# RWKV-7 attention and a squared-ReLU FFN on one core: weights rounded through PSUM with ACT's help, stores issued after their producers, the state's decay and transposes moved into the iteration before

## The chip, the cores and the metric

The kernel runs on one core of one Trainium2 chip. The metric is the device time of one launch in microseconds. The kernel before took 1444.61 us, the median of three runs (1443.46 to 1452.1). The profile is one further execution.

Engines: PE is TensorE's matmuls, PEld its weight loads, DVE is VectorE, ACT is ScalarE, POOL is GpSimd, SP is SyncE, which here only issues DMAs. A trailing q (SPq, ACTq) is an engine's own issuing of DMAs. Each engine works through its instructions strictly in the order in which the program lists them.

## The reference

```python
# attention: B=4, H=8, S=768, D=40; r, k, v, w, a, b of shape (B,H,S,D), w in 0.85..0.95
for t in range(S):
    y[:, :, t] = einsum('bhd,bhde->bhe', rt, state)          # state: (B,H,D,D), starts at 0
    Sa = einsum('bhde,bhe->bhd', state, at)
    state = state * wt[:, :, None, :] - einsum('bhd,bhe->bhde', Sa, bt)
    state = state + einsum('bhd,bhe->bhde', vt, kt)
# bridge: x = y as (B*S, H*D) = (3072, 320)
# FFN: w_in (320, 2048), w_out (2048, 320), both float64 as given
h = maximum(x @ w_in, 0.0)
out = (h * h @ w_out).astype(float32)
```

## The kernel before

*The attention in chunks.* The 768 steps are cut into 6 chunks of 128. A chunk of one batch, with its 8 heads, is a unit; `order` lists the 24 units, chunk by chunk and in each the four batches. A unit has four pieces of work, each a Python generator that yields between its steps:

- `early(i)` (through `prepare(i)`, which first issues the next unit's loads): products of the decays w in both directions (`up`, `down`), the transposed and scaled a and b, their products N. All are stored to DRAM: `kept_up`, `kept_down`, `kept_a`, `kept_d` (the diagonal blocks of N, which `solve` reads) and `kept_n`.
- `solve(c)`: POOL inverts the 64-row blocks of a whole chunk, four units at once, with 63 pairs of TENSOR_TENSOR (L298, L300), and stores the result to DRAM as `kept_t`. Its input `half_n` comes back from `kept_d`.
- `rest(i)`: loads down, aT, up of unit i and later `T` (from `kept_t`, four DMAs, L344) and `N21`; forms the masked products A and RV and the scaled k and b.
- `chain(i)`: what depends on the state. It scales the state `st` by the decays (L359 to L362, DVE), transposes it (L366, PE, into PSUM tile ps_c, copied by ACT to `sd`), multiplies through T and N (copies xr and minus_x by ACT; L378 is the first of them), grows the state, and writes y into `tokens`. Rows that don't fit are moved by small DMAs from SP, the gap copies (L428).

*The FFN.* `ffn()` takes two units of tokens as a group (12 groups): 16 w_in steps (three matmuls into PSUM ps_f, ACT Relu L445, DVE square L446) and 8 w_out steps of four matmuls each; the output is copied by ACT (`o`, L459) and stored by SP (L461).

*The weights.* They come as float64 pairs of 32-bit words, and the kernel rounds them to fp32 with integer operations: 12 wide pieces of w_in (128x512) and 16 narrow ones of w_out (128x320). `fetch_weights()` issues a piece's DMAs on ACT's queue into one of two raw buffers, `rounded()` does eight DVE instructions (L180 to L188). The wide raw buffers lie in the still unused w_out tile, so rows name that `w_out`.

*What sets the order.* Nothing is scheduled automatically: instructions stand on their engines in the order of the Python code. First come eight units of `early`, with `solve(0)` after the fourth, then most of `rest(0)`, then `run(weights(...))` with 16 pieces, `solve(1)`, and the 24 iterations. `weave` interleaves in iteration i: chain(i), rest(i+1), prepare(i+8), weights (iterations 0 and 1), and 13 steps of the FFN. After the last unit of chunk c, solve(c+2) is issued. Then the remaining FFN runs alone. The line `first = rest(0, ...)` stops `rest(0)` after six of its seven steps, so its T loads come behind the rounding in the code, though SP reaches them early.

A DMA of SP's or ACT's queue announces its landing on one of eight semaphores (DMAHW0_49 to DMAHW7_49), which the framework hands out in program order over both queues; a DMA that takes one again waits until the one that had it before has landed. PSUM has 8 buffers of 128x512: four `ps_w`, two `ps_c`, two `ps_f`.

Of the kernel before, what the change touches and what calls it, by code (L numbers as in the profile page):

```python
# [9 lines left out]
I32 = mybir.dt.int32  # L10
# [7 lines left out]
def kernel(  # L18
# [66 lines left out]

    quads = lambda t_: t_.rearrange("p (q t) -> p q t", q=NP)
# [70 lines left out]
    spare = [room[:, 2 * WI * i:2 * WI * (i + 1)] for i in range(2)]  # L157
    spare_bits = [room[:, WI * i:WI * (i + 1)].bitcast(I32) for i in (4, 5)]
    raws = [single(f"raw{i}", [128, 2 * DM]) for i in range(2)]
    raw_bits = [single(f"bits{i}", [128, DM]).bitcast(I32) for i in range(2)]  # L160
    fetched = []

    def fetch_weights():
        if not pieces:
            return
        dst, srcs, cleared = pieces.pop(0)
        wide = len(pieces) >= NF
        raw = (spare if wide else raws)[len(pieces) % 2]
        if cleared:
            nc.vector.memset(raw, 0.0)  # L170
        for row, m_, src in srcs:
            nc.scalar.dma_start(out=raw.bitcast(I32)[row:row + m_], in_=src.bitcast(I32))
        fetched.append((dst, raw, spare_bits if wide else raw_bits))

    def rounded(dst, raw, scratch):
        power, p_ = scratch
        words = raw.rearrange("p (f e) -> p f e", e=2)
        lo, hi = words[:, :, 0].bitcast(U32), words[:, :, 1].bitcast(I32)
        bits = dst.bitcast(I32)
        nc.vector.tensor_scalar(power, hi, 20, 0x7FF, Alu.logical_shift_right, Alu.bitwise_and)  # L180
# [5 lines left out]
        nc.vector.scalar_tensor_tensor(rest, lo, 2.0 ** -52, p_.bitcast(FP32), Alu.mult, Alu.mult)  # L186
        nc.vector.tensor_tensor(bits, bits, p_, Alu.bitwise_or)  # L187
        nc.vector.tensor_tensor(dst, dst, rest, Alu.add)  # L188
# [3 lines left out]
    for j in range(NT):  # L192
        for f in range(0, DFF, WI):
            srcs = [(row, n, moe_w_in[o:o + n, f:f + WI]) for j_, row, o, n in places if j_ == j]
            pieces.append((w_in[:, j, f:f + WI], srcs, f < 2 * WI and sum(n for _, n, _ in srcs) < 128))
    pieces += [(w_out[:, f, :], [(0, 128, moe_w_out[f * 128:(f + 1) * 128, :])], False) for f in range(NF)]

    def weights(n):
        for _ in range(n):
            if moe_w_in.dtype == FP32:  # L200
                if pieces:
                    dst, srcs, _ = pieces.pop(0)
                    if sum(m_ for _, m_, _ in srcs) < 128:
                        nc.gpsimd.memset(dst, 0.0)
                    for row, m_, src in srcs:
                        nc.scalar.dma_start(out=dst[row:row + m_], in_=src)
            else:
                fetch_weights()
                if fetched:
                    rounded(*fetched.pop(0))  # L210
            yield
# [36 lines left out]
    def early(i):  # L248
# [11 lines left out]
        nc.sync.dma_start(out=kept_up[i], in_=up)  # L260
        nc.sync.dma_start(out=kept_down[i], in_=down)
        yield
        bT, aT = turned("bT", 1), turned("aT", 1)
        nc.vector.tensor_tensor(bT, bT_, down[:, :, 1:C + 1], Alu.mult)
        nc.vector.tensor_tensor(aT, aT_, up[:, :, :C], Alu.mult)  # L265
        nc.sync.dma_start(out=kept_a[i], in_=aT)
        yield
        bb, c = order[i]
        for e, p_ in enumerate(products(bT, aT)):
# [3 lines left out]
            for half in range(2):  # L273
                rows = slice(half * HC, (half + 1) * HC)
                nc.sync.dma_start(out=kept_d[c][bb, half, heads].rearrange("h s t -> s h t"), in_=t_[rows, :, rows])
            nc.sync.dma_start(out=kept_n[i][:, heads, :], in_=t_[:HC, :, HC:])
# [29 lines left out]
    def rest(i, g):  # L306
# [7 lines left out]
        ends = g["ends"] = new("ends", [128, NP], 3)  # L314
        g["up"], g["aT"] = up, aT
        yield
        kT, rT = turned("kvT", 1), turned("rT", 2)
        nc.vector.tensor_tensor(kT, turn(x_["k"]), down[:, :, 1:C + 1], Alu.mult)  # L318
        nc.vector.tensor_copy(ends, down[:, :, 0])
        yield  # L320
        g["A"] = masked("A", 4, kT, aT)
# [5 lines left out]
        yield  # L327
        g["RV"] = masked("RV", 4, vT, rT)
# [4 lines left out]
        inv = p_.rearrange("t (h d) -> t h d", h=H)[:, :, :D]  # L333
        for nm in ("k", "b"):
            nc.vector.tensor_tensor(x_[nm][:, :, :D], inv, x_[nm][:, :, :D], Alu.mult)
            g[nm] = x_[nm]
        g["v"] = x_["v"]
        yield

        g["T"], g["N"] = new("T", [128, H, HC], 2), new("N21", [HC, H, HC], 2)  # L340
        nc.sync.dma_start(out=g["N"], in_=kept_n[i])
        for half in range(2):
            for par in range(2):
                nc.sync.dma_start(out=g["T"][half * HC + par:(half + 1) * HC:2],  # L344
# [222 lines left out]
```

## Time and profile before

| | |
|---|---|
| median of three runs | 1444.61 us |
| the profiled execution | 1453.09 us, span on the core 1451.4 us |
| mean granted TensorE clock | 0.808 of full |
| busy: PE | 1049.5 us (72%) |
| busy: POOL | 687.7 us (47%) |
| busy: DVE | 591.8 us (41%) |
| busy: ACT | 201.6 us (14%) |
| first solve on POOL | 57 to 175 us |
| first xr copy of the first chain | 321.94 us |
| last FFN run, nothing beside it | from 1410.39 us |

How to read it: a busy TensorE isn't one at its peak, since its matmuls take twice as long at half the granted clock. The rows called stretches below give the busy time of each engine in a stretch with the clock granted in it. A wait row reads: engine, what waited, what released it, total us, times, longest. Idle time of an engine that isn't the bottleneck costs nothing. The slices cut the span into 40 of 36 us.

### The profile page before, as it was taken

The page shows a single profiled execution, that of the slowest core. Times are in us where ns is not written, and L with a number is a line of the kernel's source. Part 1 is how long each engine was busy: PE and PEld are TensorE (multiplying, and loading weights), DVE is VectorE, ACT ScalarE, POOL GpSimd, SP SyncE. Part 2 cuts the span into 40 slices and gives each one's busy share as a digit, 9 for nine tenths or more (in the row PEclk, how much of TensorE's full clock was granted, in tenths as well). Part 3 has the DMA queues.
Part 4 walks back from the last instruction along what each step waited for, and adds up shares of the span by engine and source line. Part 5 has one row for each costly group of instructions (what it writes and reads, how often), then busy time and mean ns, then how long its engine had stood idle before and what let it go on. Part 6 is the DMA issues. An engine that isn't in the chain of part 4 may idle for free.

```text
span 1451.4 us, 18536 instructions
## 1 busy us (share of the span) xinstructions
PE 1049.5 (72%) x7248; PEld 865.5 (60%) x7248; DVE 591.8 (41%) x1095; ACT 201.6 (14%) x453; POOL 687.7 (47%) x815
## 2 busy tenths in 40 slices
PE   5340000016699689898998998989968989899999
PEld 4340000016577578676876876768757767686877
DVE  6433059998653252333332532344223123232311
ACT  1000000001022121211110211111111111121211
POOL 2399859991000099920699503997009991000000
PEclk7555555556589998998897997988898799989999
DMA  9960091103554544451744248514343133320200
GB/s 166 180 136 14 31 161 37 45 27 115 128 99 89 99 83 84 89 128 55 114 99 93 72 88 121 99 53 107 82 83 53 42 58 82 62 53 21 54 11 10
DMA packets 300104, 116.91 MB, mean 81 GB/s; under 512 B 270192, under 2 KB 275184, under 8 KB 298480
## 3 DMA queue, kind: packets, MB, share of 16 engines
q1 hardware_dynamic: 295104, 98.94, 35.6%
q10 hardware_dynamic: 4048, 10.49, 2.6%
q0 software_dynamic: 864, 6.29, 1.1%
q8 instruction: 57, 0.93, 0.3%
q14 instruction: 31, 0.25, 0.1%
HBM read 75.96 MB, written 38.73 MB: 79 GB/s over the span
## 4 chain that ended last, share of the span: by engine, by line
PE 63%; DVE 15%; POOL 8%; DMA 8%; SPq 3%; issue 2%; ACT 1%; DVEq 0%; POOLq 0%; ACTq 0%
PE ps_f L78 34%; PE ps_c L78 16%; PE ps_w L78 6%; POOL half_t L300 4%; PE ps_w L226 4%; POOL half_p L298 4%; DMA in_k<-in_k_dram 2%; DMA half_n<-kept_d 1%; DMA tokens<-tokens 1%; PE ps_c L366 1%; SPq L428 1%; DVE w_in L187 1%; DVE w_out L184 1%; DVE w_out L186 1%; DMA kept_a<-aT 1%
## 5 line engine op out<-in xcount | busy, mean ns | idle before, releaser
L298 POOL TENSOR_TENSOR half_p<-half_n,half_t 128x462 f32<-128x462 f32 (+19 forms) x378 | 316.2, 836 | 465.3 <-DMA half_n<-kept_d 436.1
L300 POOL TENSOR_TENSOR half_t<-half_t,half_p 128x462 f32<-128x462 f32 (+19 forms) x378 | 346.8, 917 | 29.6
L78 PE MATMUL ps_f<-tokens,w_in 128*128 128x256 f32 x1152 | 322.3, 427 | 25.9 <-DMA tokens<-tokens 25.3
L78 PEld LDWEIGHTS ps_f<-tokens,w_in 128*128 128x128 f32 x1152 | 232.6, 213 | 69.1 <-issue 21.4
L78 PE MATMUL ps_f<-w_out,hid 128*128 128x320 f32 x768 | 225.4, 443 | 0.0
L446 DVE TENSOR_TENSOR hid<-ps_f,hid 128x256 f32<-128x256 f32 x192 | 80.4, 420 | 350.9 <-ACT hid L445 350.9
L78 PE MATMUL ps_c<-xr,T 64*64 64x40 f32 x768 | 59.8, 239 | 216.8 <-ACT xr L378 215.0
L78 PEld LDWEIGHTS ps_c<-xr,T 64*64 64x64 f32 x768 | 54.0, 148 | 236.1 <-ACT xr L378 215.1
L78 PEld LDWEIGHTS ps_f<-w_out,hid 128*128 128x128 f32 x768 | 142.7, 193 | 56.1 <-issue 2.7
L445 ACT ACTIVATE hid<-ps_f 128x256 f32<-128x256 f32 x192 | 73.8, 384 | 377.1 <-PE ps_f L78 377.1
L78 PEld LDWEIGHTS ps_c<-in_v,A 128*128 128x128 f32 x384 | 66.0, 259 | 3.0 <-issue 0.2
L78 PE MATMUL ps_c<-in_v,A 128*128 128x40 f32 x384 | 63.0, 337 | 0.0
L318 DVE TENSOR_TENSOR kvT<-ps_w,down 128x512 f32<-128x512 f32 x24 | 16.6, 691 | 101.6 <-DMA down<-kept_down 91.5
L242 DVE TENSOR_TENSOR A<-ps_w,upper 128x512 f32<-128x512 f32 x48 | 30.9, 685 | 61.6 <-PE ps_w L78 61.6
L78 PE MATMUL ps_w<-aT,bT 40*128 40x128 f32 x384 | 35.1, 334 | 25.5 <-DVE aT L265 25.5
L366 PE MATMUL ps_c<-ident,state 128*128 128x128 f32 x80 | 17.7, 361 | 47.9 <-DVE state L362 47.9
L242 DVE TENSOR_TENSOR RX<-ps_w,upper 128x512 f32<-128x512 f32 x48 | 30.9, 685 | 51.2 <-PE ps_w L78 51.2
L378 ACT COPY xr<-ps_c 64x320 f32<-64x320 f32 x24 | 10.1, 419 | 292.9 <-DVE bits L186 220.9
L78 PEld LDWEIGHTS ps_w<-aT,bT 40*128 40x128 f32 x384 | 29.6, 230 | 32.4 <-issue 23.1
L226 PE MATMUL ps_w<-ident,in_k 128*128 128x128 f32 x96 | 20.0, 343 | 37.1 <-DMA in_k<-in_k_dram 37.1
L366 PEld LDWEIGHTS ps_c<-ident,state 128*128 128x128 f32 x80 | 11.3, 178 | 57.8 <-DVE state L362 45.6
L271 ACT COPY N<-ps_w 128x512 f32<-128x512 f32 x48 | 25.9, 589 | 137.3 <-PE ps_w L78 120.4
(184 smaller groups left out, 1325.6 us busy)
## 6 DMA issues: line engine op xcount, KB each, us to landing
kept_up<-up SPq DMA_DIRECT2D x24, 260.0 KB
kept_down<-down SPq DMA_DIRECT2D x24, 260.0 KB
down<-kept_down SPq DMA_DIRECT2D x24, 260.0 KB
up<-kept_up SPq DMA_DIRECT2D x24, 260.0 KB
kept_a<-aT SPq DMA_DIRECT2D x24, 256.0 KB
kept_d<-N SPq DMA_DIRECT2D x96, 64.0 KB
half_n<-kept_d SPq DMA_DIRECT2D x12, 512.0 KB
kept_t<-half_t POOLq DMA_DIRECT2D x6, 1024.0 KB, 4.6
```

The source lines that it names most:

```text
L78: nc.tensor.matmul(o, l_, r_, start=start, stop=True, skip_group_check=True)
L184: nc.vector.scalar_tensor_tensor(p_, hi, -(1 << 31), power, Alu.bitwise_and, Alu.bitwise_or)
L186: nc.vector.scalar_tensor_tensor(rest, lo, 2.0 ** -52, p_.bitcast(FP32), Alu.mult, Alu.mult)
L226: nc.tensor.transpose(p_[:, q * 128:(q + 1) * 128], pair(x_, q), ident)
L242: nc.vector.tensor_tensor(t_, p_, over4(upper), Alu.mult)
L271: nc.scalar.copy(t_, p_)
L298: eng.tensor_tensor(p_, ns[s // Q][:, s % Q, s % Q + 1:].unsqueeze(1).to_broadcast([128, n, m_]), ts[:, :n, s:s + 1].to_broadcast([128, n, ...
L300: eng.tensor_tensor(ts[:, :n, s + 1:], ts[:, :n, s + 1:], p_, Alu.subtract)
L318: nc.vector.tensor_tensor(kT, turn(x_["k"]), down[:, :, 1:C + 1], Alu.mult)
L366: nc.tensor.transpose(p_[:, q * 128:(q + 1) * 128], st[:, q].rearrange("p e d -> p (e d)"), ident)
L445: nc.scalar.activation(h_, p_, Act.Relu)
L446: nc.vector.tensor_tensor(h_, p_, h_, Alu.mult)
```

## The change

1. **Rounding.** Intermediate words go to PSUM (`bits` in ps_f, `low` in ps_c during the first run, in ps_f later), so that each DVE instruction has at most one input in SBUF. Six DVE instructions are left per piece; two go to ACT (L213: Relu with the bias tile `lowest`, which clamps and shifts the exponent; L214: the low word scaled by 2^-52). Four wide raw buffers instead of two; POOL clears them once. Pieces whose sources are two DMAs (j = 2) come first, and the first fetches stand ahead of rest(0)'s ACT copies. In the first run one piece's first half is issued ahead of the previous piece's second half. 12 wide and 5 narrow pieces are rounded ahead of the first chain, where it was 12 and 4; 11 are left for iterations 0 and 1.
2. **Stores.** `store()` puts a DMA into a line; `tick()`, once in each weave step, issues those that are due: one or two steps after the producer's code.
3. **State.** The decay and the transposes of the state move from chain(i)'s head to rest(i) in the iteration before. T and N are loaded earlier for the last three batches of a chunk. rest has nine steps, woven from step 2 on.
4. **FFN.** A group may start one iteration later than before: group 0 after iteration 1 as before, group g after iteration 2g+2. Iteration 4 so has no FFN, and behind the last chain stand 35 steps instead of 23.
5. **Buffers.** aT in `early` 1 to 2; A 4 to 2; f 2 to 1; end 2 to 1; ends 3 to 2; sd 1 to 2.

```diff
+    def later(fn, steps=2):
+        line.append([steps, fn])
+    def tick():
+        for entry in line:
+            entry[0] -= 1
+        while line and line[0][0] <= 0:
+            line.pop(0)[1]()
+    def store(out_, in_, steps=2):
+        later(lambda: nc.sync.dma_start(out=out_, in_=in_), steps)
...
     def fetch_weights():
...
+        while count[0] < len(pieces):
+            n = count[0]
+            wide = n < NARROW
+            if len(fetched) + len(begun) >= (4 if wide else 2) or (n >= NARROW and count[1] < NARROW):
+                return
...
+    def rounded_first(pool):
...
+        bits, low = psum(ps_f)[:, :m_], psum(pool)[:, :m_]
+        p_ = (wide_p if m_ == WI else narrow_p)[(len(begun) + count[1]) % 2]
+        nc.vector.tensor_scalar(bits.bitcast(I32), hi, 20, 0x7FF, Alu.logical_shift_right, Alu.bitwise_and)
+        nc.scalar.activation(bits.bitcast(I32), bits.bitcast(I32), Act.Relu, bias=lowest, scale=float(1 << 23))
+        nc.scalar.activation(low, lo, Act.Copy, scale=2.0 ** -52)
+    def rounded_second():
...
+        nc.vector.scalar_tensor_tensor(p_bits, hi, -(1 << 31), bits, Alu.bitwise_and, Alu.bitwise_or)
         nc.vector.tensor_scalar(bits, hi, 0xFFFFF, 3, Alu.bitwise_and, Alu.logical_shift_left)
-        nc.vector.tensor_scalar(power, power, 896.0, 1151.0, Alu.max, Alu.min)
-        nc.vector.tensor_scalar(power, power, 896.0, float(1 << 23), Alu.subtract, Alu.mult)
-        nc.vector.scalar_tensor_tensor(p_, hi, -(1 << 31), power, Alu.bitwise_and, Alu.bitwise_or)
-        rest = power.bitcast(FP32)
-        nc.vector.scalar_tensor_tensor(rest, lo, 2.0 ** -52, p_.bitcast(FP32), Alu.mult, Alu.mult)
-        nc.vector.tensor_tensor(bits, bits, p_, Alu.bitwise_or)
-        nc.vector.tensor_tensor(dst, dst, rest, Alu.add)
+        nc.vector.tensor_tensor(dst, low, p_, Alu.mult)
+        nc.vector.tensor_tensor(bits, bits, p_bits, Alu.bitwise_or)
+        nc.vector.tensor_tensor(dst, sum_, dst, Alu.add)
...
-        nc.sync.dma_start(out=kept_up[i], in_=up)
+        store(kept_up[i], up)
...
+        if c > 0:
+            st = states.tiles[bb]
+            f_ = new("f", [128, NP, 2], 1)
+            nc.vector.tensor_tensor(f_[:, :, 0], ended[bb], ends, Alu.mult)
...
+            nc.vector.tensor_tensor(st[:, :, :, :D], st[:, :, :, :D],
+                                    f_.unsqueeze(3).to_broadcast([128, NP, 2, D]), Alu.mult)
         g["RV"] = masked("RV", 4, vT, rT)
...
+        if c > 0:
+            p_ = psum(ps_c)
+            for q in range(NP):
+                nc.tensor.transpose(p_[:, q * 128:(q + 1) * 128], st[:, q].rearrange("p e d -> p (e d)"), ident)
+            sd = g["sd"] = new("sd", [128, NP, 2, DP], 2)
+            nc.scalar.copy(sd.rearrange("p q e d -> p q (e d)"), quads(p_))
+        yield
+        if bb == 0:
+            inverses()
...
+    run(weights(NARROW + NF // 4, ps_c))
+    while begun:
+        rounded_second()
...
-        if i % GB == GB - 1:
-            gathered.add(i // GB)
+        if i % GB == 0 and i > 0 or i == GB - 1:
+            gathered.add(max(i // GB - 1, 0))
+    gathered.add(len(order) // GB - 1)
```

Where the rows come to stand. First ACT's queue around the first solve: L172 (L201 after) are the DMAs that fetch weights, 40 + 40 + 24 + 16 rows to a piece or 40 + 40 for the first four after, L323/L325 (L371/L373) the copies of rest(0), L213/L214 the new rounding instructions. Before, from the copies on:

```order
L323 COPY rT<-ps_w 128x512 [waits PE_49]
L325 COPY kvT<-ps_w 128x512 [waits DVE_49,PE_49]
L172 DMA w_out<-in_moe_w_in_dram 40x1024 [waits DMAHW7_49,DVE_49]
L172 DMA w_out<-in_moe_w_in_dram 40x1024 [waits DMAHW1_49]
L172 DMA w_out<-in_moe_w_in_dram 24x1024 [waits DMAHW3_49]
L172 DMA w_out<-in_moe_w_in_dram 16x1024 [waits DMAHW5_49]
L172 DMA w_out<-in_moe_w_in_dram 40x1024 [waits DMAHW7_49,DVE_49]
L172 DMA w_out<-in_moe_w_in_dram 40x1024 [waits DMAHW1_49]
L172 DMA w_out<-in_moe_w_in_dram 24x1024 [waits DMAHW2_49]
L172 DMA w_out<-in_moe_w_in_dram 16x1024 [waits DMAHW4_49]
```

The same place now; eight DMAs of the first four pieces (40x1024) stand ahead of the copies and are not shown:

```order
L213 ACTIVATE ps_f<-ps_f,lowest 128x512 [waits DVE_49]
L214 ACTIVATE ps_c<-w_out 128x512
L201 DMA w_out<-in_moe_w_in_dram 40x1024 [waits DMAHW0_49,DVE_49,Activation_49]
L201 DMA w_out<-in_moe_w_in_dram 40x1024 [waits DMAHW2_49]
L201 DMA w_out<-in_moe_w_in_dram 24x1024 [waits DMAHW4_49]
L201 DMA w_out<-in_moe_w_in_dram 16x1024 [waits DMAHW6_49]
L213 ACTIVATE ps_f<-ps_f,lowest 128x512 [waits DVE_49]
L214 ACTIVATE ps_c<-w_out 128x512 [waits DMAHW7_49]
L201 DMA w_out<-in_moe_w_in_dram 40x1024 [waits DMAHW0_49,DVE_49,Activation_49]
L201 DMA w_out<-in_moe_w_in_dram 40x1024 [waits DMAHW2_49]
L201 DMA w_out<-in_moe_w_in_dram 24x1024 [waits DMAHW3_49]
L201 DMA w_out<-in_moe_w_in_dram 16x1024 [waits DMAHW5_49]
```

Before, the second piece's third and fourth DMAs take semaphores that T loads had; now these are the sixth piece's, and ACT's rounding instructions stand between the DMAs. SP's loads of T (from kept_t, which POOL's queue writes, DMASW0_49) and of the second solve's input, before:

```order
L344 DMA T<-kept_t_247 32x8x64 [waits DMAHW0_49,DMASW0_49]
L344 DMA T<-kept_t_247 32x8x64 [waits DMAHW2_49]
L344 DMA T<-kept_t_247 32x8x64 [waits DMAHW4_49]
L344 DMA T<-kept_t_247 32x8x64 [waits DMAHW6_49]
L293 DMA half_n_1147<-kept_d_170 64x2048 [waits DMAHW0_49,Pool_49]
```

And now:

```order
L358 DMA T<-kept_t_253 32x8x64 [waits DMAHW7_49,DMASW0_49]
L358 DMA T<-kept_t_253 32x8x64 [waits DMAHW1_49]
L358 DMA T<-kept_t_253 32x8x64 [waits DMAHW3_49]
L358 DMA T<-kept_t_253 32x8x64 [waits DMAHW5_49]
L327 DMA half_n_1189<-kept_d_176 64x2048 [waits DMAHW7_49,DMAHW2_49,Pool_49]
```

The T loads keep their place behind the first solve; which weight DMAs share a semaphore with them has moved.

The second place is TensorE between two chains in the steady stage. L366 (L398 after) are the transposes of the state; `rT,sd`, `RV` and `RX` are the last products of a unit, `in_v,A` the first of the next, `tokens,w_in` the FFN. Before:

```order
L78 MATMUL ps_c<-rT,sd 128x128 x4
L78 MATMUL ps_c<-RV,in_k_87 64x128 x8
L78 MATMUL ps_c<-RX,in_b_91 64x128 x8
L332 MATMUL ps_w<-ident,down 128x128 x4
L78 MATMUL ps_w<-aT,bT 128x128 x8
L78 MATMUL ps_f<-tokens,w_in 128x256 x3
L366 MATMUL ps_c<-ident,state_131 128x128 x4
L78 MATMUL ps_f<-tokens,w_in 128x256 x3
L78 MATMUL ps_c<-in_v_98,A 128x40 x8
L78 MATMUL ps_c<-state_131,aT__3706 128x80 x4
```

And now:

```order
L388 MATMUL ps_w<-ident,down 128x128 x4
L78 MATMUL ps_w<-aT,bT 128x128 x8
L78 MATMUL ps_f<-tokens,w_in 128x256 x3
L78 MATMUL ps_c<-rT,sd 128x128 x4
L78 MATMUL ps_c<-RV,in_k_87 64x128 x8
L78 MATMUL ps_c<-RX,in_b_91 64x128 x8
L398 MATMUL ps_c<-ident,state_131 128x128 x4
L78 MATMUL ps_f<-tokens,w_in 128x256 x9
L78 MATMUL ps_c<-in_v_98,A 128x40 x8
L78 MATMUL ps_c<-state_131,aT__3718 128x80 x4
```

The transposes of the state now close a unit's products, with nine FFN matmuls behind them, and the decay that they read is issued on DVE several steps earlier.

More of the change, by code (lines that the diff above doesn't have):

```diff
@@ L156 @@
     room = w_out.rearrange("p f c -> p (f c)")
-    spare = [room[:, 2 * WI * i:2 * WI * (i + 1)] for i in range(2)]
-    spare_bits = [room[:, WI * i:WI * (i + 1)].bitcast(I32) for i in (4, 5)]
+    wide_raws = [room[:, 2 * WI * i:2 * WI * (i + 1)] for i in range(4)]
     raws = [single(f"raw{i}", [128, 2 * DM]) for i in range(2)]
-    raw_bits = [single(f"bits{i}", [128, DM]).bitcast(I32) for i in range(2)]
-    fetched = []
-    def fetch_weights():
[L164 to L173, printed above, removed]
@@ L435, in ffn @@
         for gi in range(len(order) // GB):
[L436 removed]
+            while gi not in gathered or left() > NF:
                 yield False
@@ L448, in ffn @@
                 yield True
-            while pieces or fetched:
+            while left():
                 yield False
```

156 lines of the change are left out of this document (90 added, 66 removed).

## The prediction

> **What bounds the kernel now.** I read the slices first, then the shares of the chain that ended last.
>
> ```profile
> PE   5340000016699689898998998989968989899999
> PEclk7555555556589998998897997988898799989999
> PE 63%; DVE 15%; POOL 8%; DMA 8%; SPq 3%; issue 2%; ACT 1%; DVEq 0%; POOLq 0%; ACTq 0%
> ```
>
> There are three stages: a start in which TensorE hardly works (to slice 9, 36 us each), 24 chains that TensorE nearly fills, and an FFN tail. The waits say who holds it.
>
> ```profile
> ACT xr L378 <- DVE bits L186: 220.9, 1, 220.9
> DVE w_out L180 <- DMA w_out<-in_moe_w_in_dram: 76.8, 4, 68.2
> ```
>
> The first chain's first copy (xr) waits for the rounding of the weights, and inside it DVE waits once 68 us for a weight DMA. Busy time by stretch and the DMA issues tell why.
>
> ```profile
> 57.18:175.05 117.87, 23.66 (x136) 20.12 (x136) 30.41 (x43) 4.39 (x8) 108.06 (x126) 0.50 0.34 73
> 197.10:321.94 124.84, 0.00 (x0) 0.00 (x0) 119.69 (x107) 0.00 (x1) 116.27 (x110) 0.50 0.24 57
> ```
>
> ```profile
> 106.36 4.34 ACTq L172 DMA_DIRECT2D w_out<-in_moe_w_in_dram  x6
> 182.69 23.16 ACTq L172 DMA_DIRECT2D w_out<-in_moe_w_in_dram  x11
> 179.69 2.58 SPq L344 DMA_DIRECT2D T<-kept_t  x4
> 175.35 4.32 DMA kept_t<-half_t
> 183.02 11.63 DMA half_n<-kept_d
> 194.72 6.03 DMA w_out<-in_moe_w_in_dram
> 200.77 5.30 DMA w_out<-in_moe_w_in_dram
> ```
>
> Columns of a stretch: length, busy PE, weight load, DVE, ACT, POOL, granted clock, DMA share. Beside the first solve (57–175) DVE is busy 30 of 118 us; nearly all rounding falls beside the second (197–322, DVE 119.7 of 124.8). ACT issues six weight DMAs at 106 and the next at 182.69, right after SP's T loads, which wait for the first solve's result (written 175.35 + 4.32). In the built program ACT's seventh weight DMA waits for a completion semaphore that a T load shares (ACT's rows above). So the fetch of weights, not DVE, loses the first solve.
>
> In the steady stage I took stretches from one first xr copy to the next, and TensorE's waits between 409 and 1410 us.
>
> ```profile
> 321.94:362.28 40.34, 29.11 (x208) 26.49 (x208) 35.34 (x80) 4.51 (x9) 11.21 (x21) 0.63 0.32 109
> 362.28:409.56 47.28, 32.37 (x215) 28.77 (x216) 31.66 (x78) 4.91 (x11) 0.00 (x0) 0.61 0.50 118
> 409.56:446.85 37.29, 36.40 (x287) 30.97 (x287) 17.68 (x38) 9.41 (x22) 0.00 (x0) 0.96 0.48 91
> 446.85:497.25 50.40, 45.37 (x310) 35.47 (x310) 15.30 (x33) 7.39 (x16) 0.00 (x0) 0.93 0.44 87
> 835.33:886.33 51.00, 46.53 (x312) 37.12 (x310) 14.76 (x32) 6.90 (x15) 0.00 (x0) 0.87 0.46 92
> 886.33:934.32 47.99, 42.19 (x309) 36.09 (x308) 20.42 (x42) 9.90 (x23) 39.43 (x51) 0.89 0.62 102
> 1183.51:1219.92 36.41, 34.48 (x279) 30.04 (x279) 13.21 (x30) 8.83 (x21) 19.61 (x32) 1.00 0.23 55
> 1302.58:1346.59 44.01, 40.70 (x267) 31.30 (x267) 8.29 (x18) 5.84 (x14) 0.00 (x0) 0.91 0.17 31
> 1346.59:1380.90 34.31, 32.38 (x263) 28.10 (x263) 12.44 (x28) 8.82 (x21) 0.00 (x0) 1.00 0.16 39
> ```
>
> ```profile
> 409.56:1077.66 668.10, 602.90 (x4291) 496.88 (x4291) 244.49 (x515) 117.67 (x267) 330.81 (x390) 0.90 0.46 91
> 1077.66:1265.45 187.79, 160.21 (x1121) 131.26 (x1121) 48.36 (x100) 29.33 (x68) 108.19 (x127) 0.89 0.34 63
> ```
>
> ```profile
> PE ps_c L366 <- DVE state L362: 47.9, 20, 3.3
> PE ps_w L226 <- DMA in_k<-in_k_dram: 26.6, 5, 10.5
> PE ps_f L78 <- DMA tokens<-tokens: 24.2, 17, 3.0
> SPq L461 <- ACT o L459: 223.5, 15, 30.2
> SPq L428 <- DVE tokens L425: 102.2, 12, 24.0
> ```
>
> Iterations 2 to 15 take 668.1/14 = 47.7 us. Busy TensorE times clock is the work at full clock: 46.53 × 0.87 = 40.5 in an odd iteration, 42.19 × 0.89 = 37.5 in an even one, 39 on average. Three waits make up 98.7 us for 22 chains: the state's transposes for its decay, the k transposes for their load, the FFN for the tokens' gap copies. The last two stand behind SP, which itself stood in line for an FFN output (223.5) and for tokens (102.2). The rest of the loss is the clock, which I take to fall after such stalls.
>
> **The change, part by part.** *Rounding.* A wide piece cost eight DVE instructions:
>
> ```profile
> 190.19 0.43 DVE L180 TENSOR_SCALAR w_out<-w_out 128x512 int32<-128x512 int32 x1 [68.15 <-DMA w_out<-in_moe_w_in_dram]
> ...
> 193.84 0.69 DVE L188 TENSOR_TENSOR w_in<-w_in,w_out 128x512 f32<-128x512 f32 x1
> ...
> 266.48 1.36 DVE L180 TENSOR_SCALAR w_out<-w_out 128x512 int32<-128x512 int32 x1
> ...
> 276.32 1.43 DVE L188 TENSOR_TENSOR w_in<-w_in,w_out 128x512 f32<-128x512 f32 x1
> ```
>
> ```profile
> 98.49 1.29 DVE L242 TENSOR_TENSOR A<-ps_w,upper 128x512 f32<-128x512 f32 x2 [1.22 <-PE ps_w L78]
> L335 DVE TENSOR_TENSOR in_k<-ps_w,in_k 128x320 f32<-128x320 f32 x24 | 11.6, 481 | 3.0 <-PE ps_w L332 3.0
> L368 ACT COPY sd<-ps_c 128x512 f32<-128x512 f32 x20 | 11.7, 586 | 58.5 <-PE ps_c L366 58.5
> ```
>
> With POOL idle that is 190.19 to 194.53 = 4.3 us, beside POOL's solve 266.48 to 277.75 = 11.3 us. It becomes six DVE instructions, each with one operand in PSUM and at most one input in SBUF, and two of ACT. The nearest row is L242: PSUM and SBUF in, two in 1.29 us at 98.49, while POOL solves. So 6 × 0.65 to 0.69 = 4.0 us a wide piece and 6 × 0.48 = 2.9 a narrow one (L335); ACT's 2 × 0.59 (L368) lie beside DVE. Bounds: 4.0, and six eighths of 11.3 = 8.5 where POOL still blocks DVE. I take 4.3 with the handover to ACT, being nearest to L242.
>
> The Trainium skill, "VectorE: DVE Perf Modes", section "The perf-mode tier table", says that a PSUM operand costs a single-source fp32 instruction its double rate. L180 at 0.43 beside L188 at 0.69 agrees on the two rates. That speaks against the change: by it alone a piece costs 4.1 for 4.3 us, no gain; by the rows the gain is only what POOL takes, 11.3 against 4.3.
>
> *When pieces arrive.* Eight DMAs of the first four pieces now go out before ACT's two copies, a fifth piece follows. But the sixth piece's last two DMAs wait on semaphores of the third and fourth T loads (order rows above), and the fifth's ACT instructions stand behind them or just ahead. So I expect three or four pieces rounded beside the first solve and DVE idle again to about 183. Then the fetches alternate with half_n and in_k loads on the same semaphores: half_n lands at 183.02 + 11.63 = 194.7, so the next full fetch at about 205 (an estimate: the two chain rows of weight DMAs before ended at 200.8 and 206.1). Seven wide pieces from there: 205 + 7 × 4.3 = 235. Five narrow ones with two raw buffers wait for their own DMAs, 4.2 each: 256. First xr at **257** instead of 321.94. Bounds: 235 (fetches at 190), 298 (DVE still blocked: 205 + 7 × 8.5 + 5 × 6.8).
>
> *First iterations.* The eleven pieces left lie in iterations 0 and 1, now both beside the second solve: 42 and 44, near the 40.34 and 47.28 of the rows, since DVE (35 and 32 busy) pays less per piece. Iterations 2 and 3 hold FFN group 0: 37 (37.29 before) and 45.37 × 0.93 + 2.7 = 45. A later group now starts an iteration later, so iteration 4 has no FFN: 39 less 13 FFN steps of 6 records at 0.24 (tail, below) = 20 us of work at full clock, 40 at half; 34, between 25 and 47. Sum to there: 257 + 42 + 44 + 37 + 45 + 34 = 459.
>
> *Steady stage.* The decay's four DVE instructions go from the chain's head into the rest of the iteration before, TensorE transposes the state right behind the y products, and w_in matmuls stand between them and the chain (order rows above): the 47.9 goes. What is late next is the decay itself: it needs the chain four back, long done. Tokens are read an iteration after their gap copies: the 24.2 goes. SP issues a store one or two steps behind its producer, so loads no longer queue behind FFN output and tokens; of in_k's 26.6 I keep 3 us at each of four chunk ends, where SP has the half_n loads first. Later stores cost nothing while their readers are iterations away: the kept tiles are read at the earliest in the solve, which takes 117.87 us against some 166 for four iterations. Iterations with least trouble exceed their work by 36.41 − 34.48 = 1.9 and 34.31 − 32.38 = 1.9, and 37.29 − 36.40 × 0.96 = 2.3; with the prepared chain's waits I take 2.7. Iterations 5 to 15: 11 × (38.8 + 2.7) = 456, + 9. Iterations 16 to 19, 187.79 before: work 35.9 (160.21 × 0.89 / 4) + 2.2 = 38, × 4 = 152, + 3. Iterations 20 to 23: work 32.4 and 40.70 × 0.91 = 37.0, + 2: 4 × 36.7 = 147.
>
> *Tail.* Eleven steps of group 10 and all 24 of group 11 come behind the last chain, where 23 steps stood.
>
> ```profile
> 1394.94 4.31 PE ps_f L78 x16
> 1410.39 37.77 PE ps_f L78 x158
> ```
>
> Three w_in steps (37.77/158 × 18 records = 4.3) and eight w_out parts (two in 4.31: 17.2) are 21.5; group 11 is 37.77 + 1.4; the end after it stays 1451.40 − 1448.16 = 3.2: 64.
>
> **Sum:** 459 + 465 + 155 + 147 + 64 = 1290 of span; the profiled execution had 1453.09 for a span of 1451.40, so 1292. It stood at 1453.09/1444.61 = 1.0059 of the median: **1284 us**.
>
> **Rivals.** *A: the fetch isn't held* (10%). If the semaphores' other users have landed early, all sixteen pieces are rounded beside the first solve, and the first chain starts when T lands, about 192: 65 us less, 1219. For: five pieces are fetched without any wait on T. Against: the 68.15 us stop of before has just this cause.
>
> *B: the steady stage doesn't speed up* (20%). Other waits take the stalls' place and the clock keeps falling: iterations 5 to 19 take what they took, 11 × 47.7 = 525 for 465 and 187.79 for 155, + 93: 1376. For: odd iterations ran at 0.87 though each wait is short. Against: iteration 2, in the same code, ran at 0.96.
>
> *C: PSUM doesn't free DVE from POOL* (7%): first xr at 298, iterations 0 and 1 some 7 longer each: + 55, 1339.
>
> *D, the other side: the clock isn't granted* (3%). Iterations 0 and 1 had 0.63 and 0.61 without FFN; iteration 4 will be such again. If TensorE doesn't come out of it, 38.8/0.62 = 63 us an iteration, 19 × 21 = + 400: 1680. It decides once the mean clock in iterations 5 to 23 falls below 0.82: (1445 − 1284)/19 = 8.5 us each, 38.8/0.82 + 2.7 = 50. Against: at 409.56 the clock went from 0.61 to 0.96 within one iteration as the FFN began. The Trainium skill, "TensorE: Matmul & The Clock Gate", Part 1, has the clock at half after an idle window of about 3.4 us and full after a busy one; by that rule iteration 5 recovers at once, and the rise at 409.56 agrees.
>
> **How the numbers follow.** Forecast 60%, A 10, B 20, C 7, D 3. The range 1220 to 1380 holds the forecast, C, half of A and, since B's waits could also go in part, most of B. A measurement of this kernel can tell about 1% from no change. B and C together come within it (1376 + 55 = 1431; 0.2 × 0.07, some 2%), D alone lies beyond: faster 0.95, same 0.02, slower 0.03.
>
> **What would show it.** First xr at 250–265, DVE idle from about 130 to 183 for a weight DMA, no L398 wait of TensorE for the state, clock above 0.93 in iterations 5 to 22 at 40 to 43 us each, iteration 4 short and at a low clock, and a last FFN run of some 60 us. Wrong would make it: the first xr near 192 or 300, or steady iterations still at 47.

## The result and the profile after

The changed kernel takes **1285.57 us** (median of 4, 1281.46 to 1289.44) against 1448.36 before (the 1444.61 above was the median without a fourth run of 1456.77): ratio 0.887, 95% interval 0.8815 to 0.8925. The forecast was 1284. The profiled execution took 1286.28 us for a span of 1284.6.

The slices of the page and the chain that ended last:

```profile
PE   6422000166899498998999998999989999999998
PE 62%; SPq 6%; DMA 4%; DVE 4%; issue 1%; ACT 0%; ACTq 0%; DVEq 0%
```

The start now ends in slice 8 of 40, at 32 us a slice. DVE's 15% and POOL's 8% of the chain are down to 4% and none. Next the waits of ACT and DVE, and ACT's own issues and instructions around the stop:

```profile
ACT ps_f L213 <- DMA w_out<-in_moe_w_in_dram: 94.9, 5, 65.3
PE ps_c L78 <- DVE w_out L222: 142.5, 1, 142.5
```

```profile
115.49 0.66 ACT L213 ACTIVATE ps_f<-ps_f,lowest 128x512 int32<-128x512 int32 x1 [2.52 <-DVE ps_f L212]
116.08 0.62 ACT L214 ACTIVATE ps_c<-w_out 128x512 f32<-128x512 uint32 x1
116.85 65.14 ACTq L201 DMA_DIRECT2D w_out<-in_moe_w_in_dram  x4
182.03 0.66 ACT L213 ACTIVATE ps_f<-ps_f,lowest 128x512 int32<-128x512 int32 x1 [65.33 <-DMA w_out<-in_moe_w_in_dram]
206.14 0.66 ACT L213 ACTIVATE ps_f<-ps_f,lowest 128x512 int32<-128x512 int32 x1 [10.38 <-DMA w_out<-in_moe_w_in_dram]
255.91 0.42 ACT L423 COPY xr<-ps_c 64x320 f32<-64x320 f32 x1 [4.12 <-PE ps_c L78]
```

```profile
177.35 2.58 SPq L358 DMA_DIRECT2D T<-kept_t  x4
```

ACT rounds three pieces, issues half of the sixth piece's fetch and stands for 65 us at its third DMA; it goes on at 182.03, after the T loads that SP issued at 177.35. Behind that stop the rounding runs as forecast, the first xr copy comes at 255.91. A wide piece on DVE beside the second solve:

```profile
217.84 0.68 DVE L220 SCALAR_TENSOR_TENSOR w_out<-w_out,ps_f 128x512 int32<-128x512 int32 x1
218.56 0.69 DVE L221 TENSOR_SCALAR ps_f<-w_out 128x512 int32<-128x512 int32 x1
219.16 0.68 DVE L222 TENSOR_TENSOR w_in<-ps_c,w_out 128x512 f32<-128x512 f32 x1
219.76 0.69 DVE L223 TENSOR_TENSOR ps_f<-ps_f,w_out 128x512 int32<-128x512 int32 x1
220.48 0.69 DVE L224 TENSOR_TENSOR w_in<-ps_f,w_in 128x512 f32<-128x512 f32 x1
221.21 0.69 DVE L212 TENSOR_SCALAR ps_f<-w_out 128x512 int32<-128x512 int32 x1
```

Six instructions of 0.68 to 0.69 us, a piece every 3.97 us (221.81 to 217.84), where it was 11.3. The steady stage by stretches, from one first xr copy to the next (iterations 4, 6, 7 and 8), and from iteration 5 to 15:

```profile
419.82:471.18 51.36, 31.35 (x235) 28.54 (x236) 15.26 (x30) 5.38 (x12) 34.25 (x46) 0.63 0.69 109
513.67:555.00 41.33, 41.33 (x311) 33.04 (x310) 16.11 (x32) 7.00 (x15) 34.22 (x47) 1.00 0.49 111
555.00:596.34 41.34, 38.84 (x307) 33.84 (x307) 18.66 (x42) 9.97 (x23) 2.11 (x3) 0.96 0.47 85
596.34:646.44 50.10, 43.12 (x311) 34.22 (x310) 17.04 (x32) 7.00 (x15) 35.66 (x48) 0.93 0.66 113
471.18:937.69 466.51, 441.97 (x3389) 367.60 (x3388) 199.24 (x412) 94.87 (x213) 296.68 (x345) 0.97 0.53 101
```

Iterations 6, 10, 14, 15 and 18 to 22 have TensorE busy throughout at full clock, and most others nearly so. Where a chunk ends (iterations 4, 8, 12, 16) they take 46 to 51 us. TensorE's waits between 345 and 1245 us:

```profile
PE ps_w L260 <- DMA in_k<-in_k_dram: 25.6, 4, 7.8
PE ps_w L78 <- DVE ends L365: 8.9, 3, 6.5
PE ps_w L78 <- DVE kvT L364: 5.4, 3, 2.5
```

The state's decay and the tokens are gone from them; in_k is left, four times, once per chunk end. The last FFN run in the chain, with nothing beside it:

```profile
1215.43 2.79 PE ps_c L78 x40
1218.22 63.15 PE ps_f L78 x260
```

### The profile page after: what moved, and what is told of

Same layout as the page of the kernel before. It is cut to its first block, busy times and chain, and to the rows that moved or that the text cites. A ratio compares the mean times of both kernels' runs of the same rounds, so it can differ in the third digit from the quotient of the medians.

```text
span 1284.6 us, 18453 instructions
## 1 busy us (share of the span) xinstructions
PE 999.5 (78%) x7248; PEld 826.2 (64%) x7248; DVE 509.1 (40%) x1034; ACT 231.2 (18%) x509; POOL 671.7 (52%) x819
## 4 chain that ended last, share of the span: by engine, by line
PE 62%; SPq 6%; DMA 4%; DVE 4%; issue 1%; ACT 0%; ACTq 0%; DVEq 0%
PE ps_f L78 34%; PE ps_c L78 15%; PE ps_w L78 7%; SPq L129 4%; PE ps_w L260 4%; DMA down<-kept_down 3%; PE ps_w L388 1%; PE ps_c L441 1%; PE ps_c L398 1%; DMA in_k<-in_k_dram 1%; SPq L99 1%; DMA aT__3077<-kept_a 1%; DVE kvT L364 0%; DVE RV L276 0%; SPq L327 0%
## 5 line engine op out<-in xcount | busy, mean ns | idle before, releaser
L332 POOL TENSOR_TENSOR half_p<-half_n,half_t 128x462 f32<-128x462 f32 (+19 forms) x378 | 305.9, 809 | 340.3 <-DMA half_n<-kept_d 311.1
L334 POOL TENSOR_TENSOR half_t<-half_t,half_p 128x462 f32<-128x462 f32 (+19 forms) x378 | 337.7, 893 | 29.7
L78 PE MATMUL ps_f<-tokens,w_in 128*128 128x256 f32 x1152 | 282.8, 390 | 4.1 <-DVE w_out L222 4.1
L78 PEld LDWEIGHTS ps_f<-tokens,w_in 128*128 128x128 f32 x1152 | 211.3, 193 | 32.3 <-DVE w_out L222 4.5
L78 PE MATMUL ps_c<-in_v,A 128*128 128x40 f32 x384 | 48.6, 289 | 142.7 <-DVE w_out L222 142.5
L78 PEld LDWEIGHTS ps_c<-in_v,A 128*128 128x128 f32 x384 | 49.7, 204 | 144.7 <-DVE w_out L222 142.9
L78 PE MATMUL ps_w<-aT,bT 40*128 40x128 f32 x384 | 42.4, 355 | 9.4 <-DVE aT L299 7.9
L470 DVE TENSOR_TENSOR tokens<-ps_c,up 128x512 f32<-128x512 f32 x24 | 16.6, 691 | 77.9 <-PE ps_c L78 77.9
L78 PEld LDWEIGHTS ps_w<-aT,bT 40*128 40x128 f32 x384 | 35.9, 248 | 16.1 <-issue 6.7
L213 ACT ACTIVATE ps_f<-ps_f,lowest 128x320 int32<-128x320 int32 (+1 forms) x28 | 16.0, 572 | 163.0 <-DMA w_out<-in_moe_w_in_dram 94.9
L292 DVE RECIPROCAL down<-up 128x256 f32<-128x256 f32 x24 | 41.7, 1738 | 0.0
```

Of the source, the lines that this page charges most:

```text
L78: nc.tensor.matmul(o, l_, r_, start=start, stop=True, skip_group_check=True)
L292: nc.vector.reciprocal(down[:, :, MID + 1:C + 1], up[:, :, MID + 1:C + 1])
L332: eng.tensor_tensor(p_, ns[s // Q][:, s % Q, s % Q + 1:].unsqueeze(1).to_broadcast([128, n, m_]), ts[:, :n, s:s + 1].to_broadcast([128, n, ...
L334: eng.tensor_tensor(ts[:, :n, s + 1:], ts[:, :n, s + 1:], p_, Alu.subtract)
L470: nc.vector.tensor_tensor(t_, y_, g["up"][:, :, :C], Alu.mult)
```

## The experiments

Each time is a median of interleaved runs with the kernel before (1448 to 1452 us in those runs); the ratio is to it.

### The two halves of the change apart

`rounding_alone` puts the new rounding, with its fetches and buffers, into the kernel before; `old_rounding` undoes the same in the changed kernel. The core of the first:

```diff
                 fetch_weights()
-                if fetched:
-                    rounded(*fetched.pop(0))
+                if fetched and not begun:
+                    rounded_first(pool)
+                if fetched and pool is ps_c:
+                    rounded_first(pool)
+                if begun:
+                    rounded_second()
...
-    run(weights(len(pieces) + len(fetched) - NF))
-    run(weights(NF // 4))
+    run(weights(NARROW + NF // 4, ps_c))
```

> The kernel before with the new rounding alone (six DVE and two ACT instructions through PSUM, four wide raw buffers, 17 pieces ahead of the first chain); the steady stage, the stores and the FFN's start stay as before. Theory (two independent gains, the start worth 66 us): first xr copy at 250 to 262 us instead of 322, iterations 2 to 23 as before at 47 us, so 1448 - 66 = 1382. Rival (what the start gains is given back, since solve 1 or the loads behind the first chain bind): first xr near 257 but a time above 1420.

> The changed kernel with the rounding of before (eight DVE instructions in SBUF, two wide raw buffers, 16 pieces ahead of the first chain); all else changed. Theory (two independent gains, the steady stage worth about 96 us): first xr at 315 to 325, steady iterations at 41 to 43 us, so 1286 + 66 = 1352. Rival (the steady stage only runs well since the rounding left it, or the clock of the start carries over): iterations above 45 us and a time above 1385.

Measured: 1378.0 us (0.9509, 0.9458 to 0.956) and 1355.13 us (0.9348, 0.9287 to 0.9409). Their gains, 70 and 93 us, add up to the change's 163 (1448.4 − 1285.6). So neither half gives back what the other brings. In `rounding_alone` the first xr copy comes at 251.0 us and iterations 5 to 15 take 48 us each; TensorE waits as before:

```profile
PE ps_c L385 <- DVE state L381: 42.2, 17, 3.5
PE ps_f L78 <- DMA tokens<-tokens: 22.1, 16, 3.0
```

In `old_rounding` the first xr comes at 325.6, and iterations 5 to 15 take 42 us each.

### What holds the weights

`unheld` issues the second solve's input and the T loads of units 0 and 1 from POOL, so that SP doesn't wait for the first solve:

```diff
-                nc.sync.dma_start(out=part[par * 64:(par + 1) * 64],
+                (nc.gpsimd if c == 1 else nc.sync).dma_start(out=part[par * 64:(par + 1) * 64],
                                   in_=blocks[:, n_ * Q:(n_ + 1) * Q, n_ * Q:])
...
+    second_solve = solve(1, nc.gpsimd)
+    next(second_solve)
+    for i in range(GB):
+        early_T[i] = load_T(i, nc.gpsimd)
...
-    run(solve(1, nc.gpsimd))
+    run(second_solve)
```

> The changed kernel with the second solve's input and the T loads of the first two units issued by POOL behind the first solve, so that no weight fetch shares a completion semaphore with a DMA that waits for that solve. Theory (the shared semaphore alone holds the weights): no 65 us stop of ACT's fetches, all 17 pieces rounded by about 185 us beside the first solve, first xr at 185 to 192, the second solve some 8 us later but hidden, and 1286 - 66 = 1220. Rival (something else holds the fetch, or DVE beside POOL is the limit): first xr above 235 and 1270 to 1290.

Measured: 1224.84 us (0.8441, 0.839 to 0.8492), 61 us below the change. In the built program no weight fetch waits for a T load any more, and ACT's queue no longer stops:

```profile
116.14 1.46 ACTq L201 DMA_DIRECT2D w_out<-in_moe_w_in_dram  x4
120.16 1.46 ACTq L201 DMA_DIRECT2D w_out<-in_moe_w_in_dram  x4
171.77 0.45 ACT L214 ACTIVATE ps_c<-raw 128x320 f32<-128x320 uint32 x1
176.34 0.42 ACT L431 COPY xr<-ps_c 64x320 f32<-64x320 f32 x1 [4.13 <-PE ps_c L78]
194.31 0.42 ACT L437 COPY minus_x<-ps_c 64x320 f32<-64x320 f32 x1 [17.54 <-PE ps_c L78]
```

A piece is fetched every 4 us, the seventeenth is rounded soon after 171.8, beside the first solve. So the shared completion semaphores alone held the weights: a DMA of ACT's waited for a DMA of SP's with which it had nothing to do but the semaphore. The first xr came earlier than expected, but the second copy, which needs T, only at 194.31; so of the 80 us that the first xr gains, iteration 0 gives 16 back (55.6 us instead of 39.8). One thing said ahead of the prediction has to be put right: those semaphores are not handed out in the order of the code. The T loads stand behind these fetches in the code, yet the fetches wait for them: the eight semaphores go round in the order in which the built program lists the DMAs of both queues, and there the four T loads alternate with the four DMAs of the fifth piece.

### PSUM or fewer instructions

`words_in_sbuf`, for the wide pieces only (the narrow ones keep PSUM):

```diff
-        bits, low = psum(ps_f)[:, :m_], psum(pool)[:, :m_]
+            bits, low = ((raws[e][:, :WI] if done else
+                          w_in[:, 1, (2 * e + k_) * WI:(2 * e + k_ + 1) * WI]) for e in range(2))
```

> The changed kernel with both intermediate words of the wide pieces in SBUF instead of PSUM (they lie in weights not yet rounded and in the narrow pieces' raw buffers); six DVE and two ACT instructions as in the change. Theory (PSUM is what frees DVE from POOL): a wide piece beside a solve takes 7 to 9 us of DVE instead of 4.0, seven of them behind the first solve add 20 to 35 us, first xr at 275 to 290, time 1306 to 1320. Rival (fewer instructions and ACT's help bring the gain): first xr near 256 and 1286.

The last four wide pieces share one pair of words here and overwrite each other's, so these weights are not the reference's; the instructions and their sizes are those of the change. Measured: 1317.01 us (0.908, 0.9057 to 0.9102), first xr at 287.8. The same six instructions beside the second solve, with the tiles in SBUF:

```profile
225.78 1.39 DVE L225 SCALAR_TENSOR_TENSOR w_out<-w_out,w_in 128x512 int32<-128x512 int32 x1
227.21 1.12 DVE L226 TENSOR_SCALAR w_in<-w_out 128x512 int32<-128x512 int32 x1
228.25 1.38 DVE L227 TENSOR_TENSOR w_in<-w_in,w_out 128x512 f32<-128x512 f32 x1
229.55 1.46 DVE L228 TENSOR_TENSOR w_in<-w_in,w_out 128x512 int32<-128x512 int32 x1
231.04 1.33 DVE L229 TENSOR_TENSOR w_in<-w_in 128x512 f32<-128x512 f32 x1
232.29 1.26 DVE L217 TENSOR_SCALAR raw<-w_out 128x512 int32<-128x512 int32 x1
```

1.1 to 1.5 us instead of 0.69: some 8 us a piece. These forms aren't slow by themselves. While POOL waits between its solves, the same instruction with both words in SBUF is the faster one (first row, `words_in_sbuf`; second row, the changed kernel):

```profile
187.94 0.43 DVE L226 TENSOR_SCALAR w_in<-w_out 128x512 int32<-128x512 int32 x1
183.45 0.69 DVE L221 TENSOR_SCALAR ps_f<-w_out 128x512 int32<-128x512 int32 x1
```

So of the first xr's 66 us earlier, 32 are PSUM's (287.8 − 255.9). Some 4 of them come from the other side: the first solve starts at the same time and ends 4.4 us later (the store of its result is issued at 177.45 instead of 173.02), and the stop of the fetch with it. Some 2 are DVE's waits for ACT through the shared words (0.79 us ahead of three pieces), which the change doesn't have. The other 34 (322 − 288) are what fewer DVE instructions and the better filled fetch bring; these two were not separated. The Trainium skill, "SBUF — State Buffer", section "Who interferes with whom", says that a DVE instruction with at most one input in SBUF and outside the two-port modes doesn't contend with GpSimd, and that one with two such inputs contends with a GpSimd instruction that reads SBUF, and one in a two-port mode with GpSimd too. These rows agree with it: 0.69 with and without POOL's solve through PSUM, 1.1 to 1.5 beside the solve from SBUF.

### The FFN's lag

`no_lag`:

```diff
-        if i % GB == 0 and i > 0 or i == GB - 1:
-            gathered.add(max(i // GB - 1, 0))
-    gathered.add(len(order) // GB - 1)
+        if i % GB == GB - 1:
+            gathered.add(i // GB)
```

`no_lag_no_gap`, besides:

```diff
-        for j, row, h, d, m_ in gaps:
-            at = (h % 2) * DP + d
-            store(t_[row:row + m_, j], t_[at:at + m_, NT], 1)
```

> The changed kernel with the FFN groups free as early as before (group g after iteration 2g+1): iteration 4 has FFN again and 23 steps are left behind the last chain instead of 35. Theory of the prediction (the lag buys off the stall on the tokens' gap copies): the tail loses 22 us, iteration 4 falls from 51 to some 43 us, but TensorE's waits for tokens come back with 20 to 25 us and the clock falls after them: 1275 to 1290. Rival (that stall came from SP's queue, which the later stores have cleared): waits for tokens under 8 us and 1286 - 31 = 1255.

Measured: 1321.08 us (0.9107, 0.905 to 0.9165), slower than both theories: without the lag the change loses 35 us. TensorE waits for the tokens 30.1 us in all, and each second iteration (5, 7, 9 and so on) takes 48.7 us where those with the same matmuls took 41.3 in the change. One such place, TensorE's instructions and then stretches of 5 us:

```profile
605.72 0.67 PE L78 MATMUL ps_f<-tokens,w_in 128*128 128x256 f32 x2 [3.40 <-DMA tokens<-tokens]
607.04 1.77 PE L78 MATMUL ps_f<-tokens,w_in 128*128 128x256 f32 x4 [0.65 <-DMA tokens<-tokens]
```

```profile
602.00:607.00 5.00, 0.99 (x5) 0.38 (x3) 1.26 (x3) 0.59 (x1) 0.00 (x0) 1.00 0.24 67
607.00:612.00 5.00, 4.96 (x21) 4.68 (x21) 0.42 (x1) 0.38 (x1) 0.00 (x0) 0.53 0.65 162
612.00:617.00 5.00, 5.00 (x21) 3.99 (x20) 0.06 (x1) 0.80 (x2) 0.00 (x0) 0.50 1.17 182
617.00:622.00 5.00, 5.00 (x26) 4.45 (x26) 0.39 (x2) 0.80 (x2) 2.71 (x8) 0.60 1.43 136
```

TensorE has 1 us of work in 5, and then gets half the clock for some 14 us, from about 607.3 to 621.0 by these rows: 4 us of pause, and up to 7 us more by the slow matmuls behind it, in part in the next iteration. Behind the other long waits for tokens, some 3 us each, the half clock lasts 10 to 16 us. To see whether that pause is all, the gap copies were left out:

> The kernel without the FFN's lag (1321 us), and without the gap copies of the tokens (48 KB a group stay unmoved, so part of the FFN's input is not the reference's). Theory (the pause of TensorE at a group's start, about 4 us for the product, the tokens and their gap copies, and the half clock behind it make up the lag's worth): TensorE's waits for tokens shrink from 30 us to under 10, the iterations of 48.7 us fall to 43 to 45, time 1255 to 1285. Rival (the early start itself costs, by its other order on TensorE, ACT and DVE): 1305 to 1321.

Measured: 1256.49 us (0.8653, 0.8602 to 0.8704). The iterations of 48.7 us take 41.8, TensorE never waits for the tokens' copies. (The copies are 80 KB a group, four of 8 and 12 KB to a unit, not the 48 KB of the text above.) So the early start as such costs nothing; the pause for the copies, with the clock behind it, costs up to 65 us (1321 − 1256; SP is also spared 96 small DMAs). The lag gets 35 of it back; the other 30 (1286 − 1256) it pays itself. By the two profiles 17 us of that lie behind the last xr copy (86.3 us against 69.4), where the lag leaves 12 more FFN steps. Iteration 4 itself takes as long without FFN as with it (51.4 and 50.8 us).

### The state and the stores

`state_in_chain` has the decay and the transposes at the head of chain(i) again and not in rest(i):

```diff
+        if c > 0:
+            f_ = new("f", [128, NP, 2], 1)
...
+            sd = new("sd", [128, NP, 2, DP], 2)
+            nc.scalar.copy(sd.rearrange("p q e d -> p q (e d)"), quads(p_))
+            yield
```

`store_at_once`:

```diff
-        later(lambda: nc.sync.dma_start(out=out_, in_=in_), steps)
+        nc.sync.dma_start(out=out_, in_=in_)
```

> The changed kernel with the state's decay and transposes back at the head of the chain; all else changed. Theory (a short stall costs more than its own length, since the granted clock falls after it): TensorE waits some 2.3 us for the decay in 20 chains again (45 us) and the clock falls behind it, 1286 + 75 to 95 = 1360 to 1380. Rival 1 (it costs its own length only): 1330. Rival 2 (the FFN's lag and the later stores already cover it): 1286 to 1295.

Measured: 1333.61 us (0.9178, 0.9121 to 0.9234), 48 us more, and TensorE's wait is back:

```profile
PE ps_c L411 <- DVE state L407: 47.5, 19, 3.5
```

In sum this is the wait's own length, as the first rival has it; the forecast of 75 to 95 us falls. But the sum doesn't show that the clock cost nothing. Behind 12 of the 18 waits between 420 and 1200 us the granted clock fell to half, for about 3 us or for as long as 13; behind the six others, one of them of 3.01 us, it did not:

```profile
686.05 1.11 PE L411 MATMUL ps_c<-ident,state 128*128 128x128 f32 x4 [3.35 <-DVE state L407]
735.51 0.65 PE L411 MATMUL ps_c<-ident,state 128*128 128x128 f32 x4 [1.94 <-DVE state L407]
```

```profile
686.05:698.05 12.00, 12.00 (x44) 10.51 (x44) 0.42 (x1) 1.39 (x3) 11.14 (x12) 0.50 1.11 159
735.51:739.51 4.00, 4.00 (x16) 3.48 (x17) 0.42 (x1) 0.97 (x2) 0.00 (x0) 0.58 0.55 89
```

At the same time other waits shrank (in_k from 25.6 to 19.5 us, kvT and `ends` from 14.3 to 3.6). So 48 us is what is left of gains and losses, and its closeness to 47.5 is in part chance.

> The changed kernel with every store issued where its producer stands in the code, as before; all else changed. Theory of the prediction (SP stands behind producers, and the loads behind it come late): waits of TensorE for in_k, T or aT of 20 us and more come back, 1300 to 1330. Rival (tokens are read an iteration later and the loads have slack now): 1280 to 1292, no change.

Measured: 1284.26 us (0.8852, 0.8815 to 0.8888): no difference from the change. The later stores bring nothing here. Whether they would without the lag was not tried.

### The chunk ends

`late_half` has this on `unheld`, `late_half_alone` on the changed kernel:

```diff
-        if bb == B - 1 and c + 2 < NCH:
-            run(solve(c + 2, nc.gpsimd))
+        if bb == 0 and 0 < c < NCH - 1:
+            parts.append((issued(solve(c + 1, nc.gpsimd)), 1, 5, 6))
```

> The kernel with unheld weights (1225 us), and the loads of the later solves' input (1.5 MB) issued five steps into the next chunk's first iteration instead of ahead of that iteration's loads. Theory (at a chunk's end the in_k load stands behind the solve's input on the DMA engines, TensorE waits 6 to 8 us and then runs at half clock): the four iterations of 47 to 51 us fall to about 42, 1225 - 32 = 1193. Rival (another load is late there, or the moved transfers collide with the loads of the same iteration): 1215 to 1230.

> The changed kernel with only the later solves' input loads issued five steps into the next chunk's first iteration. Theory (what iteration 4 took above the forecast, 51 us for 34, and the 47 to 50 us of the other chunk ends are the solve's input standing ahead of that iteration's loads, not the missing FFN): iteration 4 at 35 to 38 us, the others at 38 to 42, 1286 - 45 = 1241. Rival (iteration 4 is long since it has no FFN and so a low clock): iteration 4 above 45 and 1255 to 1265.

Measured: 1172.82 us (0.8085, 0.8064 to 0.8105) and 1238.79 us (0.8532, 0.8486 to 0.8578): 52 and 47 us below the kernels that they are built on. The second meets its theory (1241), the first gains 20 us more than its theory had (1193). First SP's issues at the start of iteration 16 and TensorE's iteration 4 in the changed kernel, then iteration 4 of `late_half_alone`:

```profile
937.47 5.49 SPq L327 DMA_DIRECT2D half_n<-kept_d  x4
943.06 3.69 SPq L129 DMA_DIRECT2D in_k<-in_k_dram  x1
```

```profile
423.68 1.90 PE L78 MATMUL ps_c<-xr,T 64*64 64x40 f32 x16 [3.90 <-DMA T<-kept_t]
436.29 1.12 PE L260 MATMUL ps_w<-ident,in_k 128*128 128x128 f32 x4 [7.80 <-DMA in_k<-in_k_dram]
445.79 2.08 PE L78 MATMUL ps_w<-aT__2811,kvT 40*128 40x128 f32 x16 [6.53 <-DVE ends L365]
```

```profile
419.20:456.40 37.20, 27.50 (x236) 25.05 (x237) 13.94 (x30) 5.41 (x12) 9.12 (x19) 0.72 0.89 150
```

With 1.5 MB of half_n ahead of them, in_k and then down reach the next unit's rest late. Without, iteration 4 takes 37 us instead of 51, still without FFN and still at a low clock of 0.72.

### Both together, and T first

`best`, on `late_half`:

```diff
+    early_T[0] = load_T(0, nc.gpsimd)
     second_solve = solve(1, nc.gpsimd)
     next(second_solve)
-    for i in range(GB):
-        early_T[i] = load_T(i, nc.gpsimd)
+    early_T[1] = load_T(1, nc.gpsimd)
-    run(weights(NARROW + NF // 4, ps_c))
+    run(weights(NARROW + NF // 4 + 3, ps_c))
```

> The kernel of late_half (1173 us) with the T loads of the first unit issued ahead of the second solve's input, and three more narrow pieces rounded ahead of the first chain. Theory (the first chain's second step waited 16 us for T behind that input): T lands at about 184, iteration 0 falls from 55 to some 42 us with a first xr some 10 us later, 1173 - 5 = 1168. Rival (rounding is the bound again, or the second solve starts later): 1173 to 1180.

Measured: 1172.61 us (0.8075, 0.8028 to 0.8122), no difference from `late_half`; the expected 5 us are less than the runs' spread (1166 to 1184). The profiled execution took 1184.24 us, 12 above the median, so its stretches are not set beside the others'. In it the first xr comes at 202.3, 26 us later than in `late_half` and not some 10, and iteration 0 takes 36.7 us instead of 55.4. Whether it is so in the shorter executions, and where the 5 us went, stays open. `late_half`, 1173 us, 8.8% under the change (1172.82/1285.57), is the fastest version found here, with `best` beside it.

## Why the prediction was right

The total came out within 2 us, in part by luck. Term by term, from the stretches (first xr copy to first xr copy):

| term | forecast | measured |
|---|---|---|
| first xr copy | 257 | 255.9 |
| iterations 0 and 1 | 86 | 87.6 |
| iterations 2 and 3 | 82 | 76.3 |
| iteration 4 | 34 | 51.4 |
| iterations 5 to 15 | 465 | 466.5 |
| iterations 16 to 19 | 155 | 154.3 |
| iterations 20 to 22 | 110 | 106.3 |
| iteration 23 | 36.7 | 19.9 |
| FFN alone, to the end | 64 | 66.4 |

- *The start* was right in its mechanism: fetches held at the sixth piece until the T loads, three pieces ahead of that stop, 4.0 us a piece, PSUM operands untouched by POOL. `unheld` and `words_in_sbuf` show both causes. Rival A had the right price, 65 us for 61, for what the change does not do; C is out.
- The rule set against the change, that a PSUM operand costs the double rate, shows (L221 and L212 at 0.69 with PSUM, 0.43 for L180 in SBUF before). It took next to nothing, as the six instructions mostly lie beside a solve, where the old ones took 1.1 to 1.7.
- *The steady stage*: the direction was right, and B is out. That 466.5 meets 465 is two misses that cancel: the nine iterations of 5 to 15 without a chunk end average 40.7 us where 38.8 + 2.7 = 41.5 was forecast (6, 10 and 14 have no time above the work at all), and the two with one take 50.2 instead of 46 (41.5 and half of the 9). Two of its reasons were off as well. The state's move is worth 48 us, about the length of its wait; there the step holds. The step "SP issues a store one or two steps behind its producer, so loads no longer queue" fails: `store_at_once` is as fast. And the tokens' wait was sized at its own 24 us: without the lag it is 30 us, and with the clock behind it cost up to 65. A slip of the sum: 160.21 × 0.89 / 4 is 35.6, not 35.9, 1 us over iterations 16 to 19.
- *Iteration 4 and the chunk ends*: the term of 34 us for iteration 4 was 17 short, and the 3 us for each later chunk end too: iterations 8 and 12 took 50, some 9 more than the others. The forecast saw half_n ahead of the loads, but gave it 3 us, and not the 6 to 8 of in_k's wait with what follows it (at iteration 4 another 6.5 us for down, and the clock). It put more than half of in_k's 26.6 us down to SP's standing in line; they stayed (25.6, four times) and went only with half_n. With half_n out of the way (`late_half_alone`) iteration 4 takes 37, near the 34.
- *Iteration 23* was counted as a full one of 36.7 us, though no rest(24) lies beside it: 17 too long. That mistake and iteration 4's cancel. So do two smaller ones: the terms add up to 1290 us of span where 1284.6 was measured, and the factor of 1.0059 between profiled execution and median, which took 8 us off, was not there in the changed kernel (1286.28/1285.57). So the start and the size of the gain are understood, the 2 us are luck; the terms miss by up to 17 us.
- D's condition did show, in small: iteration 4 ran at 0.63, and the clock was back at 0.96 in iteration 5, as expected against it. It doesn't always come back that soon: in `state_in_chain` it stayed at half for some 13 us from 686 on, with TensorE busy throughout.

## What to carry to other kernels

Look through the built program for DMAs that wait on a completion semaphore shared with another queue's DMA: a fetch that needs nothing can stand 65 us behind one that waits for a solve, and no line of the code shows it. An engine's idle time in the chain is worth about its length, and a pause of TensorE, here already one of 2 us, often also the slow matmuls behind it, without a fixed price; so bulk loads with slack go behind the small loads that the next step needs. Check a sum term by term even where the total fits.

## What the runs showed of the hardware that was not expected

- The clock behind a pause: after 5 us with 1 us of matmuls TensorE ran at half clock for some 14 us, though its matmuls filled them (`no_lag`). Waits of 1.94 us were followed by half clock for about 3 us in some places and by none in others, one of 3.35 us by some 13 us, one of 3.01 us by none (`state_in_chain`). What decides between them these runs don't show.
- DVE's durations with a PSUM operand are the same to 0.01 us beside POOL's solve and without it (0.68 to 0.69 at 218 to 222 and at 183 to 186 us in the changed kernel). With the words in SBUF they are 0.43 to 0.69 without the solve and 1.1 to 1.5 beside it, and POOL pays too: its first solve takes 4.4 us longer (`words_in_sbuf`).
- The granted clock in the records of the start isn't comparable between executions: the profiled one of the change has 1.00 from the beginning (mean 0.952), its other three have means of 0.85 to 0.857 with times of 1281 to 1289. The 1.00 is not what ran: the same 16 matmuls `aT,bT` take 2.08 us at 69.07 there and 2.08 us at 69.00 in `words_in_sbuf`, whose record has 0.50 at that place; at full clock they take 1.42 us (595.18 in `no_lag`). Stretches of the start are therefore compared by length alone.
